# Attention tail keys weighted by side-by-side 64-row matmuls, one normalisation per head pair, and a new order of work inside a slot

## The chip, the cores and the metric

The kernel runs on one core of a Trainium2 chip. Its engines take instructions from queues of their own, in order, and wait for one another by semaphores: PE (TensorE, matrix multiplies, with a weight load ahead of every multiply, shown as PEld), ACT (ScalarE), DVE (VectorE), POOL (GpSimd, here only issuing loads) and SP (SyncE, here only issuing DMA transposes). The metric is the device time of one execution in microseconds; the median of 3 runs of the kernel before is 413.92 us (413.15 to 414.23).

## The reference

Eight batches, eight heads, 576 positions, head width 64. The attention has a bias that depends on the distance of two positions, and its output feeds a bilinear feed-forward layer:

```python
scores = scale * q @ k.T + bias[bucket(|i - j|), head]     # 576 x 576 for each of 64 heads
attn = softmax(scores);  o = attn @ v                      # 64 wide
x = o.transpose(0, 2, 1, 3).reshape(4608, 512)             # tokens x model
out = ((x @ w_a) * (x @ w_b)) @ w_out                      # 512 -> 1536 -> 512
```

## The kernel before

**Attention.** Heads are handled in 32 pairs p, four to a batch. The 576 positions are 4 blocks of 128 ("main") and 64 more ("tail"). Scores are computed transposed, keys on the partitions, so the result of the exponential is at once the weight operand of the product with the values. For one pair of the batches 2 to 7 (`shared(p)`, p of 8 or more) there are:

- four score tiles, t = 0 to 3 (`qk`, L415): key block t against the 512 main queries, two matmuls with 64 contraction rows each, one per head, into the two banks of one score tile; `ex` (L439, ACT) takes the exponential of 128x1024, `mul` (L444, DVE) multiplies by the exponential of the bias;
- the main keys against the 64 tail queries (`rows`, L424): 8 matmuls of 64 rows and 64 columns, head 0 into bank `trb`, head 1 into bank `qr`, in one go with the score tiles 2 and 3; `ex_rows` (L431) empties them in two ACT instructions, `mul_rows` (L539) applies the bias;
- the tail keys against all queries (`qk_tail`, L488 and L489), 512 and 128 columns wide, from an operand in which the two heads stand as diagonal blocks; `ex_tail` (L515, 128x640), `mul_tail` (L531);
- the values (`av_mm`): for each block jq of 128 queries one 130-column matmul with the tail keys of both heads (L568; the values `vt` are again diagonal blocks, padded with zeros) and eight 65-column matmuls with the main keys (L578); for the tail queries one of the first kind and four of 130 columns (L572). The 65th column of each head is ones, so the row sum of the softmax comes out beside the product. `av(p, (0, 1, 2))` and `av(p, (3, 4))` use one PSUM bank in turn, and `av_norm` (L589, L591, L596, DVE) empties it each time with a reciprocal and one to three multiplies into `XG`;
- `t_x`: two DMA transposes on SP's queue bring `XG` into `xn`, the input of the feed-forward layer.

**Feed-forward.** Nine chunks of 512 tokens, each 36 units of four 512-column matmuls: 24 units that alternate between `ff_a` (bank `pa`, emptied by ACT into `ha`, L649) and `ff_b` (bank `pb`, multiplied with `ha` into `g` by DVE, L652), then 12 units `po` (L679), three for each 128 tokens, the third followed by an ACT copy (L684) and an output DMA issued by ACT.

**Order.** `manual_schedule` keeps the instructions in the order of the Python calls. The first 8 pairs are placed by a written list of tokens (`opening`). From s = 8 on, each *slot* s makes the scores of pair s and weights the values of pair s-1; the loop puts 9 feed-forward units between its steps (each `U` in the lists `head`, `pair`, `late`, `tail` stands for one). Chunk c of batch c reads `xn` of the four pairs of batch c. Loads stand on POOL's queue (`load_half`, `load_vt`), the DMA transposes of keys, queries and `XG` on SP's.

**PSUM.** Eight banks: two score tiles of two banks (`ps_sc`, taken in turn by `qk` and `qk_tail`), one for `av` and `qr`, one for `trb`, and two taken in turn by `pa`, `pb` and `po` (`ps_ff`).

Of the kernel before, what the change touches and what calls it, by code (L numbers as in the profile page):

```python
# [13 lines left out]
def kernel(  # L14
# [19 lines left out]
    NM = 4  # L34
# [16 lines left out]
    ps_av = ctx.enter_context(tc.tile_pool(name="ps_av", bufs=1, space=bass.MemoryType.PSUM))  # L51
    ps_tr = ctx.enter_context(tc.tile_pool(name="ps_tr", bufs=1, space=bass.MemoryType.PSUM))
# [172 lines left out]
    def load_first(x, dst):  # L225
# [179 lines left out]
    def shared(p):  # L405
        return p >= 8

    def qk(p, t0, ts=None):
        qT, kT, _ = operands(p)
        st[p].setdefault("at", [None] * NM)  # L410
        for t in ts or (t0, t0 + 1):
            ps = ps_sc.tile([128, 2, 512], FP32, tag="sc", name=f"qk{p}_{t}")
            for hh in range(2):
                r = slice(64 * hh, 64 * hh + 64)
                nc.tensor.matmul(out=ps[:, hh, :], lhsT=kT[r, t, :], rhs=qT[r, :, :],  # L415
                                 start=True, stop=True)
            st[p]["ps", t] = ps
        if shared(p) and t0 == 2:
            z = operands(p)[2]
            rows = (trb.bitcast(FP32), ps_av.tile([128, 512], FP32, tag="av", name=f"qr{p}"))  # L420
            for t in range(NM):
                for hh in range(2):
                    r = slice(64 * hh, 64 * hh + 64)
                    nc.tensor.matmul(out=rows[hh][:, ST * t:ST * t + ST], lhsT=kT[r, t, :],  # L424
                                     rhs=z[r, 0, ST * hh:ST * hh + ST], start=True, stop=True)
            st[p]["rows"] = rows

    def ex_rows(p):
        st[p]["att"] = at = att[p % 2]
        for hh in (1, 0):  # L430
            nc.scalar.activation(  # L431
                out=at[:, 0:512].rearrange("p (t h c) -> p h t c", h=2, t=NM)[:, hh, :, :],
                in_=st[p]["rows"][hh][:, 0:256].rearrange("p (t c) -> p t c", t=NM),
                func=ACTF.Exp, scale=scale)
# [49 lines left out]
    def qk_tail(p):  # L484
        qT, kT, z = operands(p)
        ps = ps_sc.tile([128, 2, 512], FP32, tag="sc", name=f"qkt{p}")
        if shared(p):
            nc.tensor.matmul(out=ps[:, 0, :], lhsT=z[:, 1, :], rhs=qT[:, :, :], start=True, stop=True)  # L488
            nc.tensor.matmul(out=ps[:, 1, 0:2 * ST], lhsT=z[:, 1, :], rhs=z[:, 0, :],  # L489
                             start=True, stop=True)  # L490
            st[p]["ps"] = (ps, None)
            return
        for t in range(NM):
            nc.tensor.matmul(  # L494
                out=ps[:, 0, 2 * ST * t:2 * ST * t + 2 * ST],
                lhsT=kT[:, t, :], rhs=z[:, 0, :], start=True, stop=True)
        n = main_tail(p)
        nc.tensor.matmul(out=ps[:, 1, 0:n], lhsT=z[:, 1, :], rhs=qT[:, (SM - n) // 128:, :],
                         start=True, stop=True)
        pt = ps[:, 1, n:n + 2 * ST] if n < SM else tr_half().bitcast(FP32)[:, 0:2 * ST]  # L500
        nc.tensor.matmul(out=pt, lhsT=z[:, 1, :], rhs=z[:, 0, :], start=True, stop=True)  # L501
        st[p]["ps"] = (ps, pt)


    def main_tail(p):
        return SM // 2 if p < 4 else SM

    def ex_tail(p):
        ps, pt = st[p]["ps"]
        n = main_tail(p)  # L510
        at = att[p % 2]
        m = 512 + n
        st[p]["att"] = at
        if shared(p):
            nc.scalar.activation(out=at[:, 512:m + 2 * ST],  # L515
                                 in_=ps[:, :, :].rearrange("p a x -> p (a x)")[:, 0:SM + 2 * ST],
                                 func=ACTF.Exp, scale=scale)
            return
        if n < SM:
            m += 2 * ST  # L520
        else:
            nc.scalar.activation(out=at[:, m:m + 2 * ST], in_=pt, func=ACTF.Exp, scale=scale)
        nc.scalar.activation(out=at[:, 0:m], in_=ps[:, :, :].rearrange("p a x -> p (a x)")[:, 0:m],
                             func=ACTF.Exp, scale=scale)

    def mul_tail(p):
        if not shared(p):
            mul_rows(p)
        at, wt = st[p]["att"], Wt_sb[:, p % 4, :]
        o = 512 + main_tail(p) - 128  # L530
        nc.vector.tensor_tensor(out=at[:, o:o + 256], in0=at[:, o:o + 256], in1=wt[:, 255::-1], op=MULT)  # L531

    def mul_rows(p):
        at, w = st[p]["att"], W_sb[p % 4]
        x = at[:, 0:512].rearrange("p (t h c) -> p h t c", h=2, t=NM)
# [3 lines left out]
        nc.vector.tensor_tensor(out=x, in0=x, in1=e, op=MULT)  # L539

    def weights(p, t, hh, jq):
        if p >= 4:
# [2 lines left out]
        return st[p]["at", jq // 2, t // 2][:, hh, o:o + 128]  # L545

    def weights_last(p, t):
        return st[p]["att"][:, 2 * ST * t:2 * ST * t + 2 * ST]

    def weights_tail(p, jq):  # L550
        if jq == 4:
# [4 lines left out]
        o = 512 + 128 * (jq if p >= 4 else jq - 2)  # L556
        return st[p]["att"][:, o:o + 128]

    def av(p, jqs):
        av_mm(p, jqs)  # L560
        av_norm(p, jqs)

    def av_mm(p, jqs, pool=None, tag="av"):
        b, hp = divmod(p, 4)
        i = b % 2
        pav = (pool or ps_av).tile([128, 3, 2, Dh + 1], FP32, tag=tag, name=f"av{p}_{jqs[0]}")
        for slot, jq in enumerate(jqs):
            nc.tensor.matmul(out=pav[:, slot, :, :], lhsT=weights_tail(p, jq),  # L568
                             rhs=vt[i][:, :, hp, :], start=True, stop=True)
# [146 lines left out]
    nxt = 0  # L716
# [151 lines left out]
    for s in range(8, NP + 1):  # L868
        new = s < NP
        U = "unit"  # L870
        A = lambda *jq: (lambda: av(s - 1, jq) if s > 8 else None)
        steps = []
        if new:
            steps += [lambda: (qk(s, 0), ex(s, 0))]
        if new:
# [3 lines left out]
            if s == 8:  # L879
                late = [U]  # L880
# [3 lines left out]
            if s % 4 == 0:  # L884
                steps += head + late + [U] + pair + [lambda: mul(s, 3)] + tail
            else:
                steps += head + pair + late + [U, lambda: mul(s, 3)] + tail
# [57 lines left out]
```

## Time and profile before

| | |
|---|---|
| median of 3 runs | 413.92 us |
| profiled execution: span, first to last instruction | 412.1 us |
| PE busy | 401.5 us, 97% |
| ACT busy, DVE busy | 252.0 us (61%), 240.6 us (58%) |
| POOL busy | 131.4 us (32%) |
| TensorE clock granted, mean | 1.000 |
| the same point of two slots, four slots apart (chain: 215.84 and 259.85) | 44.01 us, so 11.00 a slot |

A busy engine says little about which one sets the end. The chain that ended last names the work that did. In the timeline the start of the next matmul group is the usable number: matmuls are pipelined, each record includes some 0.17 us of tail that overlaps its follower. On ACT and DVE the same holds: starts, not durations, give the rate at which a queue empties.

### The profile page before, as it was taken

How to read it: one execution, taken by the hardware profiler on the slowest of the kernel's cores; microseconds unless marked ns; L12 is line 12 of the kernel's file. 1: busy time of each engine (PE TensorE's matmuls, PEld its weight loads, DVE VectorE, ACT ScalarE, POOL GpSimd, SP SyncE). 2: the span in 40 equal slices, each digit the busy share in tenths (PEclk: the TensorE clock that was granted, in tenths of full speed). 3: DMA queues.
4: the chain of work that ended last, by engine and by line, in shares of the span. 5: the costliest groups of instructions: out<-in, count | busy, mean ns of one | idle time of the engine just before them, and what ended most of it. 6: DMA issues, size and time to landing. Idle time of an engine off the chain costs nothing.

```text
span 412.1 us, 8718 instructions
## 1 busy us (share of the span) xinstructions
PE 401.5 (97%) x3420; PEld 209.6 (51%) x3471; DVE 240.6 (58%) x568; ACT 252.0 (61%) x386; POOL 131.4 (32%) x188
## 2 busy tenths in 40 slices
PE   7999999999999999999999999999999999999996
PEld 3476656455554555455445555555445454444443
DVE  4799997366755765476646764567547652421320
ACT  5898992577748665667557765767476642322321
POOL 5966466887029400960069004300000000000000
PEclk9999999999999999999999999999999999999999
DMA  9999999999969924994199908960520012002004
GB/s 152 185 204 197 206 137 148 166 184 131 91 127 157 141 40 91 151 127 94 35 159 150 120 17 136 117 92 17 117 67 17 16 40 78 0 5 98 2 2 102
DMA packets 135962, 42.36 MB, mean 103 GB/s; under 512 B 113544, under 2 KB 131176, under 8 KB 135920
## 3 DMA queue, kind: packets, MB, share of 16 engines
q0 software_dynamic: 81120, 19.88, 54.9%
q1 hardware_dynamic: 49456, 12.61, 19.9%
q10 hardware_dynamic: 5344, 9.31, 7.1%
q8 instruction: 27, 0.44, 0.5%
q14 instruction: 15, 0.12, 0.1%
HBM read 39.23 MB, written 9.45 MB: 118 GB/s over the span
## 4 chain that ended last, share of the span: by engine, by line
PE 95%; DMA 1%; ACT 1%; issue 1%; DVE 0%; ACTq 0%; SPq 0%
PE pb L642 23%; PE pa L642 23%; PE po L679 22%; PE av L578 8%; PE qk L415 7%; PE av L568 2%; PE av L572 2%; PE qkh L455 1%; PE qkt L488 1%; DMA xn<-in_k_dram 1%; PE trb L330 1%; PE trb L424 1%; PE trk L330 1%; ACT ath L461 0%; PE qkt L494 0%
## 5 line engine op out<-in xcount | busy, mean ns | idle before, releaser
L439 ACT ACTIVATE at<-qk 128x1024 bf16<-128x1024 f32 x112 | 113.4, 1029 | 27.4 <-DMA out_dram<-ob 10.3
L652 DVE TENSOR_TENSOR g<-pb,ha 128x512 bf16<-128x512 f32 (+1 forms) x114 | 75.6, 663 | 74.8 <-PE pb L642 58.5
L642 PE MATMUL pb<-xn,wb 128*128 128x512 bf16 (+1 forms) x440 | 111.1, 368 | 0.8
L642 PE MATMUL pa<-xn,wa 128*128 128x512 bf16 (+1 forms) x440 | 110.8, 368 | 0.7
L649 ACT ACTIVATE ha<-pa 128x512 f32<-128x512 f32 (+1 forms) x114 | 66.3, 581 | 67.6 <-PE pa L642 63.8
L679 PE MATMUL po<-wo,g 128*128 128x512 bf16 x403 | 95.5, 379 | 0.8
L444 DVE TENSOR_TENSOR at<-at,W 128x1024 bf16<-128x1024 bf16 x112 | 75.0, 685 | 22.4 <-ACT at L439 22.3
L642 PEld LDWEIGHTS <-wa 128*128 128x128 bf16 x456 | 41.2, 98 | 46.6 <-issue 6.8
L642 PEld LDWEIGHTS <-wb 128*128 128x128 bf16 x456 | 40.6, 98 | 42.9 <-issue 4.7
L679 PEld LDWEIGHTS <-g 128*128 128x128 bf16 x420 | 38.8, 98 | 44.9 <-issue 2.5
L684 ACT ACTIVATE ob<-po 128x512 f32<-128x512 f32 x34 | 20.4, 600 | 40.2 <-PE po L679 30.1
L578 PE MATMUL av<-vm,at 128*128 128x65 bf16 x896 | 41.2, 193 | 0.0
L578 PEld LDWEIGHTS <-at 128*128 128x128 bf16 x896 | 37.4, 97 | 6.1
L174 POOL DMA_DIRECT2D vt<-in_v_dram x12 | 7.4, 622 | 101.9 <-PE av L572 101.1
L136 POOL DMA_DIRECT2D qn<-in_q_dram x48 | 36.6, 825 | 9.2 <-PE trb L501 6.9
L589 DVE RECIPROCAL rc<-av 128x6 f32<-128x6 f32 (+1 forms) x64 | 11.9, 186 | 45.7 <-PE av L578 41.1
L145 POOL DMA_DIRECT2D kn<-in_k_dram x48 | 36.2, 800 | 2.6 <-DMA qn<-in_q_dram 1.6
L568 PE MATMUL av<-vt,att 128*128 128x130 bf16 x152 | 33.6, 221 | 0.2
L415 PE MATMUL qk<-QB,KB 64*128 64x512 bf16 x192 | 29.1, 381 | 0.3
L591 DVE TENSOR_TENSOR XG<-av,rc 128x384 bf16<-128x384 f32 (+2 forms) x64 | 27.2, 425 | 2.2
L515 ACT ACTIVATE att<-qkt 128x640 bf16<-128x640 f32 x24 | 16.8, 701 | 13.0 <-PE qkt L489 13.0
L568 PEld LDWEIGHTS <-att 128*128 128x128 bf16 x152 | 14.9, 98 | 6.4
(105 smaller groups left out, 322.8 us busy)
## 6 DMA issues: line engine op xcount, KB each, us to landing
out_dram<-ob ACTq DMA_DIRECT2D x31, 256.0 KB, 2.9
vn<-in_v_dram POOLq DMA_DIRECT2D x16, 256.0 KB, 5.7
kn<-in_k_dram POOLq DMA_DIRECT2D x48, 64.0 KB, 4.9
qn<-in_q_dram POOLq DMA_DIRECT2D x48, 64.0 KB, 4.1
wa<-in_moe_w_a_dram POOLq DMA_DIRECT2D x3, 512.0 KB, 8.9
wb<-in_moe_w_b_dram POOLq DMA_DIRECT2D x3, 512.0 KB, 8.3
wo<-in_moe_w_out_dram POOLq DMA_DIRECT2D x1, 1536.0 KB, 15.7
xn<-XG SPq DMA_TRANSPOSE x52, 3.5
```

Of the source, the lines that this page charges most:

```text
L136: nc.gpsimd.dma_start(out=by_tile(qn[b % 2])[:, h0 // 4, t, :, :], in_=q[b, h0:h1, 128 * t:128 * t + 128, :].transpose([1, 0, 2]))
L145: nc.gpsimd.dma_start(out=by_tile(kn[b % 2])[:, h0 // 4, t, :, :], in_=k[b, h0:h1, t:SM:NM, :].transpose([1, 0, 2]))
L415: nc.tensor.matmul(out=ps[:, hh, :], lhsT=kT[r, t, :], rhs=qT[r, :, :], start=True, stop=True)
L439: nc.scalar.activation(out=at[:, :, :], in_=ps[:, :, :], func=ACTF.Exp, scale=scale)
L444: nc.vector.tensor_tensor(out=at[:, :, :], in0=at[:, :, :], in1=w[:, :, S - 1 + t:S - 1 + t - SM:-1], op=MULT)
L568: nc.tensor.matmul(out=pav[:, slot, :, :], lhsT=weights_tail(p, jq), rhs=vt[i][:, :, hp, :], start=True, stop=True)
L578: nc.tensor.matmul(out=pav[:, slot, hh, :], lhsT=weights(p, t, hh, jq), rhs=vm[i][:, 2 * hp + hh, t, :], start=False, stop=True, skip_grou ...
L591: nc.vector.tensor_tensor(out=xg[:, jqs[0]:jqs[0] + m, :, :], in0=pav[:, 0:m, :, 0:Dh], in1=rc[:, 0:m, :].unsqueeze(3).to_broadcast([128, ...
L642: nc.tensor.matmul(out=ps[:, 0:n], lhsT=w[df // 4][:, mc, 128 * (df % 4):128 * (df % 4) + 128], rhs=xn_sb[mc][:, 512 * c + lo:512 * c + lo ...
L649: nc.scalar.activation(out=ha[:, 0:n], in_=ff["pa", df, lo][:, 0:n], func=ACTF.Copy)
L652: nc.vector.tensor_tensor(out=g_sb[df][:, lo:lo + n], in0=ff["pb", df, lo][:, 0:n], in1=ff["ha", df, lo][:, 0:n], op=MULT)
L679: nc.tensor.matmul(out=po[:, :], lhsT=g_sb[df][:, 128 * tt:128 * tt + 128], rhs=wo_sb[:, df, :], start=(df == 0), stop=(df == NDF - 1))
```

## The change

In batches 2 to 7:

- The tail keys' weighting no longer uses diagonal blocks of values. The tail values are loaded compactly into `vc` (head 0 on partitions 0 to 63, head 1 on 64 to 127). For each of the five query blocks two 65-column matmuls with 64 contraction rows, one per head, write the two banks of the new tile `xb`. The main keys follow with 40 matmuls of 65 columns, in the order t, query block, head, alternating between the banks. One `av_out` empties both banks: one reciprocal, one multiply of 128x512, two small ones.
- The tail keys against the tail queries are computed with the `rows`, which become ten matmuls of 64 rows into the two banks of `xb` ahead of the weighting, and move from the second pair of score tiles to the first. `ex_rows` is one ACT instruction of 128x640, `ex_tail` shrinks to 128x512.
- `xb` takes the place of the `av` and `trb` banks everywhere.
- The slot is put in another order: scores 0 and 1 with the rows, three units, tail scores, one unit, scores 2 and 3, and directly behind them the weighting of pair s-1 as a whole, then five units. Slot 8 takes 6 units in place of 9, so every chunk starts three units later in its slot.

```diff
+    vc = [wpool.tile([128, H // 2, Dh + 1], BF16, name=f"vc{i}") for i in range(2)]
...
     def load_vt(b):
         for hh in range(2):
             nc.gpsimd.dma_start(
-                out=vt[b % 2][64 * hh:64 * hh + 64, hh, :, 0:Dh],
+                out=vc[b % 2][64 * hh:64 * hh + 64, :, 0:Dh],
...
+    xb = ps_x.tile([128, 2, 512], FP32, tag="xb", name="xb")
+    trb = xb[:, 0, :].bitcast(BF16)
...
-        if shared(p) and t0 == 2:
+        if shared(p) and t0 == 0:
             z = operands(p)[2]
-            rows = (trb.bitcast(FP32), ps_av.tile([128, 512], FP32, tag="av", name=f"qr{p}"))
-            for t in range(NM):
+            for t in range(NM + 1):
                 for hh in range(2):
                     r = slice(64 * hh, 64 * hh + 64)
-                    nc.tensor.matmul(out=rows[hh][:, ST * t:ST * t + ST], lhsT=kT[r, t, :],
+                    nc.tensor.matmul(out=xb[:, hh, ST * t:ST * t + ST],
+                                     lhsT=z[r, 1, :] if t == 0 else kT[r, t - 1, :],
                                      rhs=z[r, 0, ST * hh:ST * hh + ST], start=True, stop=True)
...
+        nc.scalar.activation(
+            out=at[:, SM:].rearrange("p (t h c) -> p h t c", h=2, t=NM + 1),
+            in_=xb[:, :, 0:320].rearrange("p h (t c) -> p h t c", t=NM + 1),
+            func=ACTF.Exp, scale=scale)
...
             nc.tensor.matmul(out=ps[:, 0, :], lhsT=z[:, 1, :], rhs=qT[:, :, :], start=True, stop=True)
-            nc.tensor.matmul(out=ps[:, 1, 0:2 * ST], lhsT=z[:, 1, :], rhs=z[:, 0, :],
-                             start=True, stop=True)
...
+    xav = xb[:, :, 0:5 * (Dh + 1)].rearrange("p h (j x) -> p h j x", j=5)
+
+    def av_tails(p):
+        b, hp = divmod(p, 4)
+        for jq in range(5):
+            for hh in range(2):
+                r = slice(64 * hh, 64 * hh + 64)
+                nc.tensor.matmul(out=xav[:, hh, jq, :], lhsT=st[p]["att"][r, 128 * jq:128 * jq + 128],
+                                 rhs=vc[b % 2][r, hp, :], start=(jq == 0), stop=True,
+                                 skip_group_check=True)
+
+    def av_main(p):
+        b, hp = divmod(p, 4)
+        for t in range(NM):
+            for jq in range(5):
+                for hh in range(2):
+                    nc.tensor.matmul(out=xav[:, hh, jq, :],
+                                     lhsT=weights(p, t, hh, jq) if jq < 4 else weights_last(p, t),
+                                     rhs=vm[b % 2][:, 2 * hp + hh, t, :], start=False, stop=True,
+                                     skip_group_check=True)
+
+    def av_out(p):
+        rc = wrk.tile([128, 2, 5], FP32, tag="rc", name=f"rc{p}")
+        xg = XG[p % 2]
+        nc.vector.reciprocal(out=rc[:, :, :], in_=xav[:, :, :, Dh])
+        nc.vector.tensor_tensor(
+            out=xg[:, 0:4, :, :].rearrange("p j h d -> p h j d"), in0=xav[:, :, 0:4, 0:Dh],
+            in1=rc[:, :, 0:4].unsqueeze(3).to_broadcast([128, 2, 4, Dh]), op=MULT)
+        for hh in range(2):
+            rows = slice(ST * hh, ST * hh + ST)
+            nc.vector.tensor_tensor(
+                out=xg[0:ST, 4, hh, :], in0=xav[rows, hh, 4, 0:Dh],
+                in1=rc[rows, hh, 4:5].to_broadcast([ST, Dh]), op=MULT)
...
-            head = [U, lambda: ex(s, 1), A(0, 1, 2), U, lambda: mul(s, 0), U,
-                    lambda: mul(s, 1)]
-            late = [A(3, 4), lambda: t_x(s - 1), U]
...
-            pair = [lambda: v_next(s), lambda: (qk(s, 2), ex(s, 2), ex_rows(s)), U,
-                    lambda: ex(s, 3), U, lambda: mul(s, 2), lambda: mul_rows(s)]
-            tail = [lambda: (qk_tail(s), ex_tail(s)), U, U, lambda: mul_tail(s)]
...
+            def second():
+                qk(s, 2)
+                if s > 8:
+                    av_tails(s - 1)
+                ex(s, 2)
+                if s > 8:
+                    av_main(s - 1)
...
+            steps += [lambda: (qk(s, 0), ex(s, 0)), U, lambda: ex(s, 1), U,
+                      lambda: (ex_rows(s), mul(s, 0)), U,
+                      lambda: (qk_tail(s), ex_tail(s), mul(s, 1)), U,
+                      lambda: mul_rows(s), second, U,
+                      lambda: (finish(), ex(s, 3)), U, lambda: (away(), mul_tail(s)), U,
+                      lambda: mul(s, 2), lambda: v_next(s), U, lambda: mul(s, 3), U]
...
-        quota = 9
+        quota = 6 if s == 8 else 9
```

`finish` is `av_out(s - 1)`, `away` is `t_x(s - 1)`. The last slot, s = 32, has no scores: the weighting of pair 31 stands alone ahead of two units.

More of the change, by code (lines that the diff above doesn't have):

```diff
@@ L50 @@
     ps_sc = ctx.enter_context(tc.tile_pool(name="ps_sc", bufs=2, space=bass.MemoryType.PSUM))
-    ps_av = ctx.enter_context(tc.tile_pool(name="ps_av", bufs=1, space=bass.MemoryType.PSUM))
-    ps_tr = ctx.enter_context(tc.tile_pool(name="ps_tr", bufs=1, space=bass.MemoryType.PSUM))
+    ps_x = ctx.enter_context(tc.tile_pool(name="ps_x", bufs=1, space=bass.MemoryType.PSUM))
     ps_ff = ctx.enter_context(tc.tile_pool(name="ps_ff", bufs=2, space=bass.MemoryType.PSUM))
@@ L219, in pad_ones @@
         nc.vector.memset(vm[i][:, :, :, Dh:Dh + 1], 1.0)
+        nc.vector.memset(vc[i][:, :, Dh:Dh + 1], 1.0)
     def pad_x(i, eng):
@@ L241, with warm_up @@
                             op=mybir.AluOpType.subtract)
-    warm = ps_av.tile([128, 512], FP32, tag="av", name="warm")
-    def warm_up(n, dst=None):
+    xb = ps_x.tile([128, 2, 512], FP32, tag="xb", name="xb")
+    trb = xb[:, 0, :].bitcast(BF16)
+    def warm_up(n):
         for _ in range(n):
-            nc.tensor.matmul(out=(warm if dst is None else dst)[:, :], lhsT=zero_sb[:, 0:128],
+            nc.tensor.matmul(out=xb[:, 1, :], lhsT=zero_sb[:, 0:128],
                              rhs=zero_sb[:, :], start=True, stop=True)
@@ L309 @@
     st = [dict() for _ in range(NP)]
-    trb = ps_tr.tile([128, 1024], BF16, tag="tr", name="trb")
     turn = [0]
@@ L417, in qk @@
             st[p]["ps", t] = ps
-        if shared(p) and t0 == 2:
+        if shared(p) and t0 == 0:
             z = operands(p)[2]
-            rows = (trb.bitcast(FP32), ps_av.tile([128, 512], FP32, tag="av", name=f"qr{p}"))
-            for t in range(NM):
+            for t in range(NM + 1):
                 for hh in range(2):
                     r = slice(64 * hh, 64 * hh + 64)
-                    nc.tensor.matmul(out=rows[hh][:, ST * t:ST * t + ST], lhsT=kT[r, t, :],
+                    nc.tensor.matmul(out=xb[:, hh, ST * t:ST * t + ST],
+                                     lhsT=z[r, 1, :] if t == 0 else kT[r, t - 1, :],
                                      rhs=z[r, 0, ST * hh:ST * hh + ST], start=True, stop=True)
-            st[p]["rows"] = rows
     def ex_rows(p):
         st[p]["att"] = at = att[p % 2]
[L430 to L434, printed above, removed]
+        nc.scalar.activation(
+            out=at[:, SM:].rearrange("p (t h c) -> p h t c", h=2, t=NM + 1),
+            in_=xb[:, :, 0:320].rearrange("p h (t c) -> p h t c", t=NM + 1),
+            func=ACTF.Exp, scale=scale)
     def ex(p, t):
@@ L514, in ex_tail @@
         if shared(p):
-            nc.scalar.activation(out=at[:, 512:m + 2 * ST],
-                                 in_=ps[:, :, :].rearrange("p a x -> p (a x)")[:, 0:SM + 2 * ST],
-                                 func=ACTF.Exp, scale=scale)
+            nc.scalar.activation(out=at[:, 0:SM], in_=ps[:, 0, :], func=ACTF.Exp, scale=scale)
             return
@@ L529, in mul_tail @@
         at, wt = st[p]["att"], Wt_sb[:, p % 4, :]
-        o = 512 + main_tail(p) - 128
+        o = (0 if shared(p) else 512) + main_tail(p) - 128
         nc.vector.tensor_tensor(out=at[:, o:o + 256], in0=at[:, o:o + 256], in1=wt[:, 255::-1], op=MULT)
@@ L534, in mul_rows @@
         at, w = st[p]["att"], W_sb[p % 4]
-        x = at[:, 0:512].rearrange("p (t h c) -> p h t c", h=2, t=NM)
+        o = last_rows(p)
+        x = at[:, o:o + 512].rearrange("p (t h c) -> p h t c", h=2, t=NM)
         rev = w[:, :, ST - 1::-1]
@@ L539, in mul_rows, with last_rows @@
         nc.vector.tensor_tensor(out=x, in0=x, in1=e, op=MULT)
+    def last_rows(p):
+        return SM + 2 * ST if shared(p) else 0
     def weights(p, t, hh, jq):
@@ L547, in weights_last @@
     def weights_last(p, t):
-        return st[p]["att"][:, 2 * ST * t:2 * ST * t + 2 * ST]
+        o = last_rows(p) + 2 * ST * t
+        return st[p]["att"][:, o:o + 2 * ST]
     def weights_tail(p, jq):
@@ L557, in weights_tail @@
         return st[p]["att"][:, o:o + 128]
-    def av(p, jqs):
-        av_mm(p, jqs)
-        av_norm(p, jqs)
+    xav = xb[:, :, 0:5 * (Dh + 1)].rearrange("p h (j x) -> p h j x", j=5)
[28 more added lines that the diff above has]
+                in1=rc[rows, hh, 4:5].to_broadcast([ST, Dh]), op=MULT)
     def av_mm(p, jqs, pool=None, tag="av"):
@@ L565, in av_mm @@
         i = b % 2
-        pav = (pool or ps_av).tile([128, 3, 2, Dh + 1], FP32, tag=tag, name=f"av{p}_{jqs[0]}")
+        if pool is None:
+            pav = xb[:, 1, 0:6 * (Dh + 1)].rearrange("p (j h x) -> p j h x", j=3, h=2)
+        else:
+            pav = pool.tile([128, 3, 2, Dh + 1], FP32, tag=tag, name=f"av{p}_{jqs[0]}")
         for slot, jq in enumerate(jqs):
@@ L763, in step @@
         if token[0] == "w":
-            warm_up(int(token[-1]), ps_av.tile([128, 512], FP32, tag="av", name=f"fill{nxt}")
-                    if token[1] == "a" else None)
+            warm_up(int(token[-1]))
             return
@@ L870, with finish, away @@
         U = "unit"
-        A = lambda *jq: (lambda: av(s - 1, jq) if s > 8 else None)
         steps = []
         if new:
-            steps += [lambda: (qk(s, 0), ex(s, 0))]
-        if new:
-            head = [U, lambda: ex(s, 1), A(0, 1, 2), U, lambda: mul(s, 0), U,
-                    lambda: mul(s, 1)]
-            late = [A(3, 4), lambda: t_x(s - 1), U]
-            if s == 8:
-                late = [U]
-            pair = [lambda: v_next(s), lambda: (qk(s, 2), ex(s, 2), ex_rows(s)), U,
-                    lambda: ex(s, 3), U, lambda: mul(s, 2), lambda: mul_rows(s)]
-            tail = [lambda: (qk_tail(s), ex_tail(s)), U, U, lambda: mul_tail(s)]
[L884 to L887, printed above, removed]
+            def second():
[5 more added lines that the diff above has]
+                    av_main(s - 1)
+            def finish():
+                if s > 8:
+                    av_out(s - 1)
+            def away():
+                if s > 8:
+                    t_x(s - 1)
+            steps += [lambda: (qk(s, 0), ex(s, 0)), U, lambda: ex(s, 1), U,
[4 more added lines that the diff above has]
+                      lambda: mul(s, 2), lambda: v_next(s), U, lambda: mul(s, 3), U]
         else:
             ff["late"] = True
-            steps += [A(0, 1, 2), U, U, U, A(3, 4), lambda: t_x(s - 1, (0, 1, 2)), U, U, U,
+            steps += [lambda: (av_tails(s - 1), av_main(s - 1)), U, U, lambda: av_out(s - 1), U,
+                      lambda: t_x(s - 1, (0, 1, 2)), U, U, U,
                       lambda: t_x(s - 1, (3, 4)), U, U, U]
```

## The prediction

> **What bounds the kernel now.** I read the page first, then the chain that ended last, then PE's timeline over one slot, then ACT and DVE beside it.
>
> From the page, busy time and the chain:
>
> ```profile
> PE 401.5 (97%) x3420; PEld 209.6 (51%) x3471; DVE 240.6 (58%) x568; ACT 252.0 (61%) x386; POOL 131.4 (32%) x188
> ...
> PE 95%; DMA 1%; ACT 1%; issue 1%; DVE 0%; ACTq 0%; SPq 0%
> ```
>
> PE is the bound, and not on average alone. Its timeline over slot 21 (start, length, engine, line):
>
> ```profile
> 215.23 0.60 PE L415 MATMUL qk<-QB,KB 64*128 64x512 bf16 x4
> 215.77 1.04 PE L642 MATMUL pa<-xn,wa 128*128 128x512 bf16 x4
> 216.64 0.22 PE L568 MATMUL av<-vt,att 128*128 128x130 bf16 x1
> 216.70 0.42 PE L578 MATMUL av<-vm,at 128*128 128x65 bf16 x8
> 216.96 0.22 PE L568 MATMUL av<-vt,att 128*128 128x130 bf16 x1
> ...
> 217.59 1.02 PE L642 MATMUL pb<-xn,wb 128*128 128x512 bf16 x4
> 218.45 1.03 PE L642 MATMUL pa<-xn,wa 128*128 128x512 bf16 x4
> 219.41 0.61 PE L415 MATMUL qk<-QB,KB 64*128 64x512 bf16 x4
> 219.85 0.19 PE L424 MATMUL trb<-ZB,KB 64*128 64x64 bf16 x1
> ...
> 220.07 1.04 PE L642 MATMUL pb<-xn,wb 128*128 128x512 bf16 x3
> ...
> 222.18 0.40 PE L572 MATMUL av<-vm,att 128*128 128x130 bf16 x4
> 222.41 1.02 PE L642 MATMUL pb<-xn,wb 128*128 128x512 bf16 x4
> ```
>
> Starts give the prices. A unit: 218.45 - 217.59 = 0.86. A pair of 64-row score matmuls side by side costs one 512-column stream, 0.86/4 = 0.215. Going over to 64 rows costs 0.10 (219.41 - 218.45 - 0.86), going back 0.11 (215.77 - 215.23 - 0.43). The eight rows: 220.07 - 219.85 - 0.11 = 0.11, or 0.03 a pair. A 130-column matmul 0.06, eight of 65 columns 0.26, so 0.0325 each; the four of L572 0.23. The slot: nine units 7.78, scores with switches 1.28, rows 0.11, weighting 0.95 + 0.61 = 1.56, tail scores 0.27: 11.00, the measured slot. No stall is left in it, so PE work removed counts fully, and so does every new PE wait.
>
> The other engines, same window and the opening:
>
> ```profile
> 24.78 0.38 PE L494 MATMUL qkt<-ZB,KT 128*128 128x128 bf16 x4 [0.53 <-ACT ath L461]
> ...
> 214.58 0.70 ACT L515 ACTIVATE att<-qkt 128x640 bf16<-128x640 f32 x1
> 215.33 0.60 ACT L684 ACTIVATE ob<-po 128x512 f32<-128x512 f32 x1
> 215.96 0.34 ACTq L687 DMA_DIRECT2D out_dram<-ob  x1
> 216.35 1.02 ACT L439 ACTIVATE at<-qk 128x1024 bf16<-128x1024 f32 x1 [0.41 <-PE pa L642]
> 217.27 0.59 ACT L649 ACTIVATE ha<-pa 128x512 f32<-128x512 f32 x1
> 217.74 1.03 ACT L439 ACTIVATE at<-qk 128x1024 bf16<-128x1024 f32 x1
> 218.72 0.69 DVE L652 TENSOR_TENSOR g<-pb,ha 128x512 bf16<-128x512 f32 x1
> 219.33 1.29 DVE L444 TENSOR_TENSOR at<-at,W 128x1024 bf16<-128x1024 bf16 x2
> ```
>
> On ACT a score exponential holds the queue 0.90 to 0.92 (216.35 to 217.27; I use 0.90), `ha` 0.47, `ob` with its DMA issue 1.02; the result is ready after the full 1.02 or 0.6. The new ex_rows (640 elements, row 0.70) I let hold it 0.60, the new ex_tail (512 elements) end after 0.60 like `ha`. DVE's `g` holds its queue 0.61. ACT starts 0.20 after PE's stream ends, DVE 0.27 (217.59 + 0.86 to 218.72). PE resumes about 0.06 after what it waited for (the exponential ahead of 24.78 ended at 24.73).
>
> **The change, part by part.**
>
> *PE work.* Per pair, before: weighting 1.56, tail scores 0.27, rows 0.11, together 1.94. After: 40 matmuls of 65 columns at 0.0325 = 1.30; ten 64-row ones, priced as the rows, five pairs at 0.03 = 0.15; tail scores 0.215; rows five pairs 0.14; together 1.80. The stretches of 64 rows stay two per slot, since the tails follow score tile 3. So 0.14 less, 24 pairs: -3.4; pair 31 has a stretch of its own, +0.2: -3.2. Bounds: 65 columns at the stream's rate are 0.027, -5 us more (23 x 40 x 0.0055); at the weight loads' rhythm (eight in 0.35, the last 0.098 long: 0.036) +3. Tails that do not run together cost 10 x 0.0325, +4. I take 0.0325 and 0.03: same widths, same two banks as the rows.
>
> The Trainium skill, TensorEngine Tiling, Instruction Overhead, says each matmul carries some 60 cycles. By that the nine matmuls more per pair would cost, at an estimated 2.4 columns a ns from the 512-column row, 9 x 0.025 = 0.22 a pair and turn the saving into a loss of 2 us. The row says 0.0325 for 65 columns, hardly above streaming; the row decides.
>
> *ACT and DVE work.* ACT loses one instruction per pair, DVE one reciprocal and one multiply. Neither is on the chain; costed at nothing where it shortens, but the order of their queues now matters:
>
> *New wait 1, score tile 3.* Tiles are taken in turn: 0, 1, tail scores, 2, 3. Tile 3 needs the bank of the tail scores, so `ex_tail` must be done. Before, the tail scores came last in the slot, with two units before their bank's next user. Now one unit and tile 2 lie between. With no stall PE would be (from the slot's start) at: score pairs 0.10 to 0.53, rows to 0.66, units to 3.36, tail scores 3.58, unit 4.44, tile 2 at 4.54, tile 3 at 4.75. ACT, by s modulo 4 (a chunk's 36 units start with the fourth of slots 1):
> - slot 0 (nine `po`): ex 0.51 and 1.41, ex_rows 2.31, then `ob` of the third unit 3.56 plus 1.02, ex_tail 4.58 to 5.18: tile 3 at 5.24, stall 0.49.
> - slot 1: `ob` of the last slot first (0.20 to 1.22), ex 1.22, 2.12, ex_rows 3.02, `ob` 3.62, ex_tail 4.64 to 5.24: 0.55.
> - slot 2: ex 0.51, `ha` must wait for its unit, 1.84; ex 2.31, ex_rows 3.21, `ha` 3.81, ex_tail 4.28 to 4.88: 0.18.
> - slot 3: `ha` of the last slot 0.20, ex 0.67, 1.57, `ha` of unit two 2.70, ex_rows 3.17, ex_tail 3.93 (tail scores end 3.73, 0.15 late by wait 2) to 4.53: none.
>
> Queued behind on PE: the tails, the weighting, five units.
>
> *New wait 2, the two `ff` banks.* `pb` of one `ff_b` is free 0.86 + 0.27 + 0.69 + 0.06 = 1.88 after its start. Two units back to back take 1.73, so an unbroken run of a, b, a, b stalls by 0.16 each time. Before, attention matmuls break every run in this slot after two units (the `pb` at 222.41 and the next, at 224.41, are 2.0 apart). Now units five to nine run unbroken, and DVE has the whole `av_out` in the middle: reciprocal 0.23, multiply of 512 elements some 0.69 (row of 384: 0.56), two of 0.21, and mul_tail 0.20, then `g`: 0.36 in place of 0.16 at the next one. Slot 1 (units five, seven, nine are `pb`): 0.16 + 0.36; slot 2 (six, eight): 0.16; slot 3 (one, three, five, seven, nine): 0.16 + 0.16 + 0.36; slot 0: none.
>
> Stalls: slot 1 1.07, slot 2 0.34, slot 3 0.68 (six each), slot 0 0.49 (five): 12.5 + 2.5 = +15.0. Bounds: zero release time -3, another 0.10 in each release and 0.10 more in ex_rows +3.
>
> *Other moves.* The rows wait for `xb`, freed by av_out at about 10.1 of the slot before, 1.8 ahead; the tails wait for ex_rows (at most 3.7, needed at 5.0): covered. `t_x` moves later: XG is ready near 8.6, its two DMA transposes (SP, 1.2 each, 3.5 to land) bring pair 4c+3 to about 12.2; the chunk starts three units into the next slot, at 14: covered by 2. SP's key and query transposes behind it are wanted two slots later. On POOL `load_vt` waits for the last weighting of its old buffer, now some 2 us later in the slot, with `load_half` behind it, wanted two slots later; batches 2 and 3 no longer wait. The 6 units in slot 8 move three to the end: the same PE work. The two small memsets: under 0.2.
>
> *Sum.* 412.1 - 3.2 + 15.0 = 423.9 for the profiled execution; 1.8 lie between its span and the median shown: 425.7.
>
> **Rivals.**
> 1. *Side by side fails* (or the bank-alternating order runs slower): +4 to +7, 430 to 433. For: no row has this operand mix. Against: the rows write two banks at 0.03 a pair. 11%.
> 2. *Faster.* The ACT queue reaches ex_tail before PE needs the bank and `g` keeps up: only -3.2 stays, 410.7. It decides where the stalls fall below 3.2 us, 0.14 a slot; wait 1 alone would need ex_tail 0.3 earlier in three slots of four. Against: the spacings above, and `ob`, which cannot start before its unit ends. 9%.
> 3. *The wait moves to `xn`.* Were XG's transposes 2 us later than reckoned, each of seven chunks would stall; 1 us each makes 433. Against: the median landing of 3.5. 5%.
> 4. *No change:* stalls of just 2 to 4.5 us cancel the saving. 3%.
>
> **How the numbers follow.** The forecast has 72%, its own range 419 to 431 (bounds -3 to -7, +3 to +5). Reaching to rival 1, with rival 2 left out: 417 to 433. A difference of 0.3% (1.2 us) is about what a measurement of this kernel can tell from none: faster 9%, same 3%, slower 88%.
>
> **What would show it.** The page: PE busy share falls to 93 or 94%. Four slots last 46.0 us. The waits list PE on ex_tail's ACT line, some 7 us, and `pb` on DVE's `g`, some 8 us; weighting of one pair, tails and main, 1.45 from its start to the next unit. Wrong: a slot of 10.9 without these waits, or 40 matmuls that take far from 1.3.

## The result and the profile after

The changed kernel takes 437.93 us (median of 4, 437.13 to 440.38) against 413.76 before: 1.0589 times as long, interval 1.0558 to 1.062. The forecast was 425.7, range 417 to 433. The direction was right; the time lies 12.2 us above the forecast and 4.9 above the range.

The page of the changed kernel: busy times, the span in 40 slices for PE and for the clock granted to it (tenths, 9 is 90% or more), and the chain that ended last. The second fence is PE's row of slices in the kernel before.

```profile
PE 411.4 (94%) x3711; PEld 208.4 (48%) x3711; DVE 235.0 (54%) x522; ACT 251.4 (58%) x362; POOL 131.3 (30%) x188
...
PE   6878889999999999999999999999999999999996
...
PEclk9789899999999999999999999999999999999999
...
PE 75%; ACT 10%; DVE 8%; issue 4%; DMA 1%; ACTq 1%; SPq 0%; DVEq 0%
```

```profile
PE   7999999999999999999999999999999999999996
```

PE's share of the chain fell from 95 to 75%; ACT and DVE hold 18% of it. The rows of slices say more: in the changed kernel slices 2 to 6 (11 to 65 us, the opening) are no longer full, and the clock sags there. The forecast had only the slots behind the opening in view.

PE's timeline of the changed kernel over slot 21 (start, length, engine, line, operands, count, and in brackets the idle time before it and what ended it), and the start of slot 25:

```profile
231.07 0.60 PE L416 MATMUL qk<-QB,KB 64*128 64x512 bf16 x4
...
235.53 0.39 PE L416 MATMUL qk<-QB,KB 64*128 64x512 bf16 x2
236.27 0.39 PE L416 MATMUL qk<-QB,KB 64*128 64x512 bf16 x2 [0.36 <-ACT att L512]
236.49 0.33 PE L566 MATMUL xb<-vc,att 64*128 64x65 bf16 x10
236.75 0.42 PE L575 MATMUL xb<-vm,at 128*128 128x65 bf16 x8
...
237.98 1.02 PE L675 MATMUL pb<-xn,wb 128*128 128x512 bf16 x4
238.85 1.03 PE L675 MATMUL pa<-xn,wa 128*128 128x512 bf16 x4
239.86 1.02 PE L675 MATMUL pb<-xn,wb 128*128 128x512 bf16 x4
240.72 1.03 PE L675 MATMUL pa<-xn,wa 128*128 128x512 bf16 x4
242.12 1.02 PE L675 MATMUL pb<-xn,wb 128*128 128x512 bf16 x4 [0.37 <-DVE g L685]
243.08 0.60 PE L416 MATMUL qk<-QB,KB 64*128 64x512 bf16 x4
...
277.14 0.60 PE L416 MATMUL qk<-QB,KB 64*128 64x512 bf16 x4
```

Four slots last 277.14 - 231.07 = 46.07 us (forecast 46.0, before 44.01). Both new waits are in this slot. Score tile 3 (the `qk` at 236.27) starts 0.74 after tile 2 (235.53), where 0.215 would do: 0.52 late. The two `pb` at 239.86 and 242.12 come 1.01 and 1.40 after the `pa` ahead of them, where 0.86 would do: 0.15 and 0.54 late. Of these 1.21 us the brackets hold only 0.73, so here the sum of the listed waits understates the stall, and the differences of the starts are used below.

Where the 24.4 us between the two profiled spans (436.5 and 412.1) arise can be read off the starts of slots 8 and 9, before (first fence) and after (second):

```profile
73.72 0.61 PE L415 MATMUL qk<-QB,KB 64*128 64x512 bf16 x4
...
83.17 0.61 PE L415 MATMUL qk<-QB,KB 64*128 64x512 bf16 x4
```

```profile
85.59 0.61 PE L416 MATMUL qk<-QB,KB 64*128 64x512 bf16 x4
...
92.86 0.61 PE L416 MATMUL qk<-QB,KB 64*128 64x512 bf16 x4
```

| | before | after | difference |
|---|---|---|---|
| opening, up to slot 8 | 73.72 | 85.59 | +11.87 |
| slot 8 (9 units before, 6 after) | 9.45 | 7.27 | -2.18 |
| slot 9 to the end | 328.93 | 343.64 | +14.71 |

The three units that slot 8 gives up (2.6 us) are done at the end, so the slots proper cost 12.1 more. The forecast was 11.8 for everything. The other half of the loss lies in the opening, in which the order of the tokens is the same in both kernels.

PE's largest waits in the changed kernel (total us, times, longest); of the last three the kernel before has none:

```profile
PE pb L675 <- DVE g L685: 4.5, 12, 0.4
PE qk L416 <- ACT att L512: 3.9, 12, 0.4
PE xb L601 <- ACT QT L321: 2.2, 2, 1.8
...
PE xb L601 <- DVE ZB L323: 1.3, 1, 1.3
...
PE xb L601 <- DVE xn L323: 0.7, 1, 0.7
```

L601 is the first matmul of the weighting in the opening; it reads `vt` and `att` and writes bank 1 of `xb`. `QT`, `ZB` and `xn` (L321, L323) are copies out of the transposes, which stand in bank 0. The matmul needs none of them. What they share with it is the tile: they read its other bank.

The same tokens on PE and DVE, after (first fence, around 28 us) and before (second, around 25 us):

```profile
27.15 0.28 PE L651 MATMUL xb<-cn_sb,XG 128*128 128x128 bf16 x2 [1.08 <-DVE XG L624]
27.61 0.48 DVE L323 COPY xn<-xb 128x256 bf16<-128x256 bf16 x2
28.14 0.22 PE L601 MATMUL xb<-vt,att 128*128 128x130 bf16 x1 [0.71 <-DVE xn L323]
```

```profile
25.20 0.29 PE L618 MATMUL trb<-cn_sb,XG 128*128 128x128 bf16 x2
25.32 0.22 PE L568 MATMUL av<-vt,att 128*128 128x130 bf16 x1
25.66 0.48 DVE L322 COPY xn<-trb 128x256 bf16<-128x256 bf16 x2
```

Before, the weighting follows the transposes after 0.12 us and without a wait, and their copy runs beside it. After, it starts 0.99 us behind them, when that copy is done (27.61 + 0.48 = 28.09).

### The profile page after: what moved, and what is told of

Its sections match the earlier page's. It is cut to its first block, busy times and chain, and to the rows that moved or that the text cites. A ratio compares the mean times of both kernels' runs of the same rounds, so it can differ in the third digit from the quotient of the medians.

```text
span 436.5 us, 9203 instructions
## 1 busy us (share of the span) xinstructions
PE 411.4 (94%) x3711; PEld 208.4 (48%) x3711; DVE 235.0 (54%) x522; ACT 251.4 (58%) x362; POOL 131.3 (30%) x188
## 3 DMA queue, kind: packets, MB, share of 16 engines
HBM read 39.23 MB, written 9.45 MB: 112 GB/s over the span
## 4 chain that ended last, share of the span: by engine, by line
PE 75%; ACT 10%; DVE 8%; issue 4%; DMA 1%; ACTq 1%; SPq 0%; DVEq 0%
PE po L712 20%; PE pb L675 18%; PE pa L675 15%; PE xb L575 7%; PE qk L416 6%; ACT at L438 3%; ACT att L512 2%; DVE g L685 2%; DVE XG L584 2%; PE xb L611 2%; DMA xn<-in_k_dram 1%; PE qkh L454 1%; ACT ob L717 1%; ACT att L430 1%; ACT ha L682 1%
## 5 line engine op out<-in xcount | busy, mean ns | idle before, releaser
L438 ACT ACTIVATE at<-qk 128x1024 bf16<-128x1024 f32 x112 | 110.2, 1024 | 20.0 <-PE qk L416 16.3
L675 PEld LDWEIGHTS <-wb 128*128 128x128 bf16 x456 | 42.3, 98 | 57.0 <-issue 16.7
L174 POOL DMA_DIRECT2D vc<-in_v_dram x12 | 7.5, 670 | 116.2 <-PE xb L566 115.5
L416 PE MATMUL qk<-QB,KB 64*128 64x512 bf16 x192 | 32.3, 382 | 4.2 <-ACT att L512 3.9
L575 PE MATMUL xb<-vm,at 128*128 128x65 bf16 x768 | 32.0, 194 | 0.0
L575 PEld LDWEIGHTS <-at 128*128 128x128 bf16 x768 | 29.1, 97 | 1.3
L575 PE MATMUL xb<-vm,att 128*128 128x65 bf16 x192 | 21.4, 193 | 0.0
L416 PEld LDWEIGHTS <-KB 64*128 64x128 bf16 x192 | 7.1, 94 | 29.6 <-issue 28.8
L583 DVE RECIPROCAL rc<-xb 128x10 f32<-128x10 f32 x24 | 5.2, 215 | 25.8 <-PE xb L575 25.8
L512 ACT ACTIVATE att<-qkt 128x512 bf16<-128x512 f32 x24 | 14.5, 606 | 4.8 <-PE pa L675 2.5
L460 ACT ACTIVATE ath<-qkh 128x1024 bf16<-128x1024 f32 x16 | 15.8, 1029 | 2.5 <-PE qkh L454 2.3
```

Source lines behind the costliest of these rows:

```text
L438: nc.scalar.activation(out=at[:, :, :], in_=ps[:, :, :], func=ACTF.Exp, scale=scale)
L512: nc.scalar.activation(out=at[:, 0:SM], in_=ps[:, 0, :], func=ACTF.Exp, scale=scale)
L575: nc.tensor.matmul(out=xav[:, hh, jq, :], lhsT=weights(p, t, hh, jq) if jq < 4 else weights_last(p, t), rhs=vm[b % 2][:, 2 * hp + hh, t, : ...
L675: nc.tensor.matmul(out=ps[:, 0:n], lhsT=w[df // 4][:, mc, 128 * (df % 4):128 * (df % 4) + 128], rhs=xn_sb[mc][:, 512 * c + lo:512 * c + lo ...
```

## The experiments

**Theory A:** half of the loss comes from the opening, where one tile of two banks has taken the place of two tiles of one bank each, so that users of one bank wait for users of the other. **Rival B:** the opening is late for another reason (the tail values loaded differently, ten matmuls more in the queue, the slower clock itself). **Theory C:** the slots cost what the forecast says, by the two waits it names and nothing else.

### Two tiles in the opening

```diff
-    xb = ps_x.tile([128, 2, 512], FP32, tag="xb", name="xb")
-    trb = xb[:, 0, :].bitcast(BF16)
...
+    warm = ps_av.tile([128, 512], FP32, tag="av", name="warm")
+    trb = ps_tr.tile([128, 1024], BF16, tag="tr", name="trb")
...
-            pav = xb[:, 1, 0:6 * (Dh + 1)].rearrange("p (j h x) -> p j h x", j=3, h=2)
+            pav = ps_av.tile([128, 3, 2, Dh + 1], FP32, tag=tag, name=f"av{p}_{jqs[0]}")
...
     pad_tl(1)
+    first.close()
...
+    xb = ps_x.tile([128, 2, 512], FP32, tag="xb", name="xb")
+    trb = xb[:, 0, :].bitcast(BF16)
```

> The changed kernel, but the opening (pairs 0 to 7) has its two PSUM banks as two tiles again, and the joint tile begins with slot 8. Theory A (joining the two banks in one tile made transposes and weighting of the opening wait for one another; the slots are as forecast): the first scores of slot 8 start near 73.7 us again in place of 85.6, the slots keep 46.1 us per four, the time is 437.9 - 12 = 426 us. Rival B (the opening is slower for another reason, such as the two added memsets, the earlier loads of the tail values or a colder clock by itself): the start of slot 8 stays above 82 us and the time above 434 us.

429.03 us (427.09 to 431.16), ratio to before 1.037 (1.0332 to 1.0409): 8.9 less than the changed kernel. PE's timeline of this kernel, from slot 8 to the start of slot 9 and the starts of slots 21 and 25, and one-microsecond windows of it (width and busy us of PE, PEld, DVE, ACT, POOL with instruction counts, then PE's granted clock, DMA share, GB/s):

```profile
73.17 0.60 PE L418 MATMUL qk<-QB,KB 64*128 64x512 bf16 x4
76.82 0.20 PE L426 MATMUL xb<-ZB 64*128 64x64 bf16 x2 [3.05 <-DMA ZB<-tl]
...
84.86 0.60 PE L418 MATMUL qk<-QB,KB 64*128 64x512 bf16 x4
...
223.39 0.61 PE L418 MATMUL qk<-QB,KB 64*128 64x512 bf16 x4
...
269.75 0.61 PE L418 MATMUL qk<-QB,KB 64*128 64x512 bf16 x4
```

```profile
77.00:78.00 1.00, 0.67 (x12) 0.36 (x6) 0.05 (x2) 0.70 (x1) 0.98 (x2) 0.50 1.90 180
...
79.00:80.00 1.00, 1.00 (x3) 0.30 (x2) 0.00 (x0) 0.00 (x0) 1.00 (x2) 0.50 2.00 199
```

Slot 8 starts at 73.17: the opening's whole loss is gone, and so are the waits on `xb` in it. But slot 8 itself now lasts 11.69 us in place of 7.27. The change has moved the row scores to the first score pair; they need the DMA transpose of the tails, which lands 3 us after PE asks for it. In the changed kernel PE's rows do not wait for it: the late opening covered that wait. In this execution the clock then stood at 0.50 from 77 to 80. So the gain was 8.9 and not 12: the cure of one wait uncovered another.

Between the two profiles the opening is 12.4 us shorter, slot 8 4.4 longer and the rest 0.9 longer. The last is a miss of its own: the slots were to keep 46.1 us for four, and those from 21 to 24 take 269.75 - 223.39 = 46.36. In slots 13, 21 and 29 tile 3 starts 1.03 after tile 2, where the changed kernel has 0.74 or 0.75. In slot 21 ACT begins its first exponential 1.39 us after the slot's start, in the changed kernel 1.12; why is not known.

### The other direction: one tile in the opening of the kernel before

```diff
-    warm = ps_av.tile([128, 512], FP32, tag="av", name="warm")
...
+    xb = ps_x.tile([128, 2, 512], FP32, tag="xb", name="xb")
+    trb = xb[:, 0, :].bitcast(BF16)
+    ps_av = None
...
-        pav = (pool or ps_av).tile([128, 3, 2, Dh + 1], FP32, tag=tag, name=f"av{p}_{jqs[0]}")
+        if pool is None and ps_av is None:
+            pav = xb[:, 1, 0:6 * (Dh + 1)].rearrange("p (j h x) -> p j h x", j=3, h=2)
+        else:
+            pav = (pool or ps_av).tile([128, 3, 2, Dh + 1], FP32, tag=tag, name=f"av{p}_{jqs[0]}")
...
     pad_tl(1)
+    first.close()
+    ps_av = ctx.enter_context(tc.tile_pool(name="ps_av", bufs=1, space=bass.MemoryType.PSUM))
...
```

> The kernel before, but with one joint two-bank tile for transposes and weighting in the opening only; from slot 8 on it is as before. Theory A: the start of slot 8 moves from 73.7 to about 85.6 us, slots stay at 44.0 us per four, time 413.8 + 12 = 426 us. Rival B: no more than 1 us of difference from 413.8.

426.85 us (425.98 to 427.02), ratio 1.0312 (1.0296 to 1.0328). The starts of slots 8, 9 and 13 on PE and two of the waits of that kernel:

```profile
85.49 0.61 PE L416 MATMUL qk<-QB,KB 64*128 64x512 bf16 x4
...
94.94 0.61 PE L416 MATMUL qk<-QB,KB 64*128 64x512 bf16 x4
...
138.96 0.61 PE L416 MATMUL qk<-QB,KB 64*128 64x512 bf16 x4
```

```profile
PE xb L572 <- ACT QT L321: 2.2, 2, 1.8
...
PE xb L572 <- DVE ZB L323: 1.2, 1, 1.2
```

Slot 8 starts 11.77 later than before (the medians differ by 13.2), the same waits stand in the list (L572 is this kernel's L601), and behind the opening nothing has changed: slots still last 44.0 for four. Theory A is shown in both directions. B falls: nothing else of the change is in this kernel. The size is good to a microsecond or two, since in the profiles of the kernels with two tiles in the opening slot 8 starts anywhere from 72.46 to 74.72.

How the 11.9 arise can be split by windows. Summed over one-microsecond windows up to slot 8, PE is idle for 4.10 us before and 12.47 after: +8.4. The rest is clock. Windows of the changed kernel:

```profile
26.00:27.00 1.00, 0.07 (x2) 0.00 (x0) 0.97 (x4) 1.00 (x2) 0.00 (x0) 1.00 1.41 163
27.00:28.00 1.00, 0.28 (x2) 0.17 (x3) 1.00 (x4) 0.52 (x1) 0.78 (x2) 1.00 1.50 200
...
29.00:30.00 1.00, 1.00 (x14) 0.70 (x13) 0.00 (x0) 0.10 (x1) 1.00 (x2) 0.61 1.08 169
30.00:31.00 1.00, 1.00 (x13) 0.42 (x10) 0.47 (x2) 0.82 (x1) 1.00 (x3) 0.50 1.27 207
```

From 26 to 28 PE works for 0.35 us; a microsecond later the clock falls to 0.50 and is full again only from 33 on. From 46 to 50 the same happens. Busy time multiplied by the missing share of the clock gives 1.7 us for each stretch, 3.4 together, and 8.4 + 3.4 = 11.8. A longer drop from 8 to 16 us is left out: the kernel of the last experiment has it too, and its slot 8 starts at 72.46. The split is an estimate from these windows and not measured by a run of its own.

### The first wait removed: tail scores one unit earlier

On top of two tiles in the opening:

```diff
-                      lambda: (ex_rows(s), mul(s, 0)), U,
-                      lambda: (qk_tail(s), ex_tail(s), mul(s, 1)), U,
+                      lambda: (qk_tail(s), ex_tail(s), ex_rows(s), mul(s, 0)), U,
+                      lambda: mul(s, 1), U,
```

> As after_split, with the tail scores one unit earlier and their exponential ahead of the rows' exponential, so that two units lie between the tail scores and the user of their bank. Theory (wait 1 of the prediction costs what was reckoned): the wait of score tile 3 goes, 6.8 us less than after_split; waits of the feed-forward banks stay, four slots last 44.6 in place of 46.1 us: about 418 us. Rival (the stall only moves to another wait, since PE is held by what DVE and ACT can deliver in a slot): under 2 us of gain.

421.72 us (419.68 to 423.43), ratio 1.019 (1.0154 to 1.0227). The starts of two slots, four apart:

```profile
217.59 0.61 PE L418 MATMUL qk<-QB,KB 64*128 64x512 bf16 x4
...
262.28 0.60 PE L418 MATMUL qk<-QB,KB 64*128 64x512 bf16 x4
```

44.69 us for four slots, and no `qk` waits for `ex_tail` any more. The kernel this one was built on takes 46.36, so its removal gains 1.67 per four slots. The forecast had 0.49 + 0.55 + 0.18 = 1.22. The 0.45 more are the tile 3 that came 0.28 later there, and one wait of `pb` of 0.16 that goes too, since the tail scores now stand ahead of that `pb`. The time is 7.3 us below that kernel's (6.8 expected); it is above the 418 expected because that kernel took 429 and not 425.

### The second wait removed: the weighting spread over the units

On top of two tiles in the opening, with the tail scores where the change has them; the ten matmuls of each key block t follow one unit each:

```diff
-    def av_main(p):
+    def av_main(p, ts=range(NM)):
...
-        for t in range(NM):
+        for t in ts:
...
                 ex(s, 2)
+                part(0)
+
+            def part(*ts):
                 if s > 8:
-                    av_main(s - 1)
+                    av_main(s - 1, ts)
...
-                      lambda: (finish(), ex(s, 3)), U, lambda: (away(), mul_tail(s)), U,
-                      lambda: mul(s, 2), lambda: v_next(s), U, lambda: mul(s, 3), U]
+                      lambda: (part(1), ex(s, 3), mul(s, 2)), U,
+                      lambda: (part(2), mul_tail(s), mul(s, 3), v_next(s)), U,
+                      lambda: (part(3), finish()), U, away, U]
```

> As after_split, with the weighting by the main keys in four parts between the units five to eight, the normalisation after the last part, and the bias multiplications of tiles 2 and 3 ahead of it. Theory (wait 2 of the prediction costs what was reckoned): the waits of pb on g fall from about 8.2 to 2.2 us, the wait of score tile 3 stays: four slots last 45.0 us, about 420 us. Rival (the breaks cost as much as they save, or the later normalisation delays the rows and the transposes): no gain on after_split, 425 us or more.

422.44 us (421.05 to 423.36), ratio 1.0217 (1.0198 to 1.0236). The same two starts, and one tile 3 between them:

```profile
217.48 0.61 PE L418 MATMUL qk<-QB,KB 64*128 64x512 bf16 x4
...
222.97 0.39 PE L418 MATMUL qk<-QB,KB 64*128 64x512 bf16 x2 [0.64 <-ACT att L514]
...
262.41 0.61 PE L418 MATMUL qk<-QB,KB 64*128 64x512 bf16 x4
```

44.93 for four, and the waits of `pb` on `g` are gone from the list, while tile 3 waits as in the kernel with two tiles. The removal gains 46.36 - 44.93 = 1.43 per four slots; the forecast had 0.52 + 0.16 + 0.68 = 1.36. The time is above the 420 expected for the reason given above; it is 6.6 us below that kernel's.

### Both waits removed

Both edits together, two tiles in the opening, and a slot 8 of 5 units that asks for its rows late:

```diff
-        if shared(p) and t0 == 0:
-            z = operands(p)[2]
+        if p > 8 and t0 == 0:
+            rows(p)
+
+    def rows(p):
+            qT, kT, z = operands(p)
...
+            if s == 8:
+                steps += [lambda: (qk(s, 0), ex(s, 0)), U, lambda: ex(s, 1), U, lambda: mul(s, 0), U,
+                          lambda: mul(s, 1), U,
+                          lambda: (qk(s, 2), ex(s, 2), rows(s), ex_rows(s)), U,
+                          lambda: (ex(s, 3), qk_tail(s), mul(s, 2), ex_tail(s), mul_rows(s), v_next(s),
+                                   mul(s, 3), mul_tail(s))]
+            else:
...
-        quota = 6 if s == 8 else 9
+        quota = 5 if s == 8 else 9
```

> The changed kernel with two separate one-bank tiles in the opening, and with both waits of the later slots removed: tail scores and their exponential one unit earlier, the weighting spread over four units so that no five units run without another step between them; slot 8 has 5 units and asks for its row scores after the second score pair, by when the transposed tails should have landed. Theory (the two waits are separate costs, 6.6 and 7.3 us as measured alone, and the cheaper weighting of 0.14 us per slot is real): slots of 43.4 us per four against 44.0 before, slot 8 starting at 73.2 and lasting under 7 us, no wait of score tile 3 on the tail exponential and none of pb on g among the larger waits, 411 us (409.5 to 413). Rival (the two waits share one cause, so that removing the second gains nothing more): slots of 44.7 per four, 417 to 418 us. Second rival (a wait takes their place, xn landing later because the normalisation comes later): slots above 44.0 with pa waiting for xn, 414 to 417 us.

411.76 us (410.73 to 412.68) against 413.64 of the kernel before: ratio 0.9955 (0.994 to 0.997), a gain of 0.45% on the kernel before, small but clear of the noise. The chain of its page, and the starts of slots 9, 20 and 24:

```profile
PE 93%; ACT 2%; DMA 1%; issue 1%; DVE 1%; ACTq 0%; SPq 0%; DVEq 0%
```

```profile
81.84 0.88 PE L418 MATMUL qk<-QB,KB 64*128 64x512 bf16 x4 [1.08 <-ACT at L443]
...
201.25 0.61 PE L418 MATMUL qk<-QB,KB 64*128 64x512 bf16 x4
...
244.46 0.61 PE L418 MATMUL qk<-QB,KB 64*128 64x512 bf16 x4
```

Four slots last 43.21 us, against 44.01 before and 43.4 expected: 10.80 a slot, in which PE's list shows no wait. Both removals together gain 46.36 - 43.21 = 3.15, alone they gained 1.67 + 1.43 = 3.10, so the two waits are separate costs. Theory C holds as to the waits; their sizes are taken up below. Only slots 9 and 13 are longer, 11.11 each. Slot 8 starts at 74.72, 1.5 later than expected, and takes 81.84 - 74.72 = 7.12, a little over what was expected, since the first scores of slot 9 wait 1.08 us for an exponential. The rival, that the second gain vanishes once the first is taken, is out, and so is the one that `xn` becomes late: `pa` is not in the list of waits.

### Is the late row score worth its place?

The same kernel, but slot 8 asks for its rows with the first score pair.

> The same as the run with both orders, but slot 8 asks for its row scores with the first score pair. Theory: they wait 2 to 3 us for the DMA transpose of the tail tile, everything behind them on TensorE waits too, and the time is 2 to 3 us above that run, 413 to 414 us, or up to 2 us more if the granted clock falls after that wait. Rival (the wait is covered elsewhere): the same time as that run.

414.1 us, in two groups: 410.51, 410.81 and 411.39, and seven times 413.27 to 415.21. The profiled execution is of the short kind: its rows start without a wait. The long ones cost some 3 us, as was expected for the median. That in them the transposed tails come late is not shown, since none was profiled; it fits that five of the seven have a mean clock of 0.995 or 0.996, as the profile with the wait of 3.05 us has (0.995). Asking later made all nine executions end by 412.68.

### Does the idle time pull the clock down?

Two tiles in the opening, and ahead of slot 8's rows:

```diff
+            if p == 8:
+                for _ in range(12):
+                    nc.tensor.matmul(out=xb[:, 1, :], lhsT=ident[:, :], rhs=W_sb[0][:, 0, 0:512],
+                                     start=True, stop=True)
```

> The changed kernel with separate tiles in the opening and 12 matmuls of 512 columns of unused data (2.6 us at the full clock) put ahead of slot 8's row scores, whose wait of 3.05 us they fill; they compute nothing that is used. Theory (the idle time itself pulls the granted clock down to 0.50 for the 3 us behind it): the clock stays at 1.00 from 73 to 85 us, slot 8 lasts 9.3 to 10 us in place of 11.69, and the time is 427 us. Rival (the clock falls for another reason there): 0.50 at 77 to 80 us again, slot 8 at 11.5 or more, 429 us or more.

428.89 us (428.31 to 430.32). PE's timeline in slot 8:

```profile
73.00 2.76 PE L425 MATMUL xb<-W,cn_sb 128*128 128x512 bf16 x12
75.69 0.20 PE L430 MATMUL xb<-ZB 64*128 64x64 bf16 x2
...
82.09 0.61 PE L418 MATMUL qk<-QB,KB 64*128 64x512 bf16 x4
```

In the profile it went as the theory says: the clock stayed at 1.00, and slot 8 took 82.09 - 72.46 = 9.63 us in place of 11.69. The median did not move (429.03 without the filler). The expected 427 was worked out from the profiled execution of the kernel without the filler, which with 431.16 was the slowest of its four; the other three had a mean clock of 0.999 or 1.000 and 427.09 to 429.11. So the drop behind that wait is a matter of single executions, and that idle time causes it is not shown by one profile with it and one without. What the median loses there is, as far as the profiles show, the wait itself: with the filler in it slot 8 still takes 9.63 us.

## Why the prediction was wrong, and what of it was right

**The step that failed** is the list of the change's parts. The sum was "412.1 - 3.2 + 15.0 = 423.9", and no term of it belongs to the opening, although the change puts `xb` in the place of the `av` and `trb` banks everywhere, the first eight pairs included. The prediction asked of `xb` only whether the rows "wait for `xb`, freed by av_out", within a slot. It looked at what the new tile holds and not at whom the old two tiles had kept apart. That term is +11.9 us (11.87 measured, 11.77 when it was put alone into the kernel before). With it the sum is 435.8 for the span, against 436.5.

**-3.2 us of PE work: right.** The ten tails take 236.75 - 236.49 = 0.26 with a switch of 0.11, so 0.15 as forecast; the forty main matmuls 237.98 - 236.75 = 1.23 (forecast 1.30), so 0.031 each. A slot without stalls is 0.20 shorter than before (10.80 and 11.00) where 0.14 was forecast, and the cheaper main matmuls are the 0.07 between. Where no wait is listed, in the kernel with both waits removed, slot 9 to the end takes 410.8 - 81.84 = 328.96 us with four units more than before (3.46), so 325.5, against 328.93: 3.4 less. Rival 1, side by side failing, is out.

The estimate that the Trainium skill's TensorEngine Tiling (Array Packing), section Instruction Overhead, led to, 0.22 more per pair from nine matmuls more, is not borne out: 0.031 us for 65 columns leaves no room for it. The estimate had added the 60 cycles to every matmul; the section's next line, that free_dim 1 has the same latency as free_dim 60, makes them a floor for narrow matmuls, and read so the page agrees with the row.

**+15.0 us of stalls: right within 2 us.** From slot 9 to the end the changed kernel takes 343.64, less 2.6 for the three units, 341.0: 15.5 above the 325.5 without stalls. By the starts of its slots 21 to 24, wait 1 is 0.52 + 0.22 + 0 + 0.48 = 1.22, just the forecast. Wait 2 is 0.69 + 0.16 + 0.86 + 0 = 1.71 and not 1.36: the simple `pb` wait is 0.15 (0.16), but the one with `av_out` in between 0.54 (0.36).

Counted by slots, stalls are 46.07 - 43.21 = 2.86 for four (2.58 forecast), or 16.7 us for slots 9 to 31, and the saving of 0.20 a slot is 4.6. Each is 1.4 to 1.7 us larger than forecast and they cancel, so that the sum agrees so well (12.1 and 11.8) is partly luck.

**What was to show it.** Four slots in 46.0: 46.07. PE busy 93 or 94%: 94%, but part of that is work at half the clock, so the agreement says little. The waits in the list were to be some 7 and 8 us; the list has 3.9 and 4.5, since it books only about half of what the starts show. Weighting of one pair in 1.45: 237.98 - 236.49 = 1.49.

**Rivals 2 and 3.** Rival 2 named the faster case as the one in which the ACT queue "reaches ex_tail before PE needs the bank and `g` keeps up", at 410.7: the kernel with both orders meets the condition, has no joint tile in the opening, and takes 411.76. Rival 3 did not occur in the changed kernel, in whose list `pa` waits for nothing; `pa` waited for `xn` for 0.5 us in all in one experiment only, the spread weighting with late tail scores.

**The three units moved out of slot 8** were costed at nothing. Slot 8 lasts 2.18 less where three units are 2.6: 0.4 us lost.

## What to carry to other kernels

List every place that uses a resource which a change replaces, not only the place for which it was made: one tile over two PSUM banks orders the users of the two banks among themselves, and in a stage that alternates between them this cost some 11.8 us here. Price a stall by the starts on a timeline against the same work without it, since the sum of the listed waits held only half of it here. Where a stage becomes faster, ask at once what the next stage finds ready: here the repaired opening ran into a transpose that its lateness had hidden.

## What the runs showed of the hardware that was not expected

- In one profile each, PE's granted clock fell to 0.50 for some 3.5 us after a wait of 3.05 us, and stayed at 1.00 after waits of 2.1 and 2.3 us (tail scores early, weighting spread). It also fell a microsecond after two microseconds that held 0.35 us of PE work. The Trainium skill, TensorE: Matmul & The Clock Gate, Part 1, names an idle window of about 3.4 us for a fall to half the rate. The rate of 0.50 agrees; here the wait was a little shorter, and in the other case scattered work did not prevent the fall.
- A drop at 8 to 16 us, in the profiles of the changed kernel, of the kernel before with one tile and of the filled one, shows no loss: the filled one has it and reaches slot 8 at 72.46, earlier than the kernel with the two tiles alone (73.17), which does not have it. Mean clocks of single executions say the same: of twenty of the kernel before, the three with 0.992 are the fastest (412.67 to 412.82 us), and of nine with both waits removed the three with 0.990 (410.73 to 410.89). Where in those the clock fell was not profiled.
